# Wide matrix products and a new order of the last rounds in an attention decode kernel

## The chip, the cores and the metric

One core of a Trainium2 chip. The metric is the device time of one launch in microseconds; lower is better. A core has a matrix engine (PE, with its weight loads shown as PEld), a vector engine (DVE), an activation engine (ACT), and a queue (SP) that issues the DMAs here. 16 DMA engines carry the data.

## What is computed

A decode step for 4 batch rows (B = 4, one token each, D = 512): a layer norm modulated by a condition, grouped-query attention over a cache, a gated residual, then a second modulated norm and a small mixing network with its own gate. All numbers are float32.

```python
mod = (_silu(c) @ w_mod).reshape(c.shape[0], 6, 1, -1)
sa, ca, ga, sb, cb, gb = ...                   # six parts of mod
h = _layernorm(x) * (1 + ca) + sa
q = (h @ wq)                                    # 32 heads of 128, 8 key heads
p = softmax(q k^T / sqrt(128))                  # 4096 cached keys per batch row and key head
x = x + ga * ((p v) @ wo)
h = _layernorm(x) * (1 + cb) + sb
u = gelu(_layernorm(h) * w1 + b1)               # 512 channels x 1792
x = x + gb * (u @ w2 + b2)
```

## The kernel before

The 4 x 8 pairs of batch row and key head make 32 *rounds* (`NS = 32`; round i belongs to batch row i // 8 and head i % 8). Each needs a key tile `k` and a value tile `v` of 2 MB, [128 x 4096] floats. All big tiles live in one ring of five places (`ring`), so a load can be issued when the tile five loads earlier has been read. SP takes the loads in program order; each waits there for its place. The last three value tiles come in pieces (`load_v`), the last in four. The output projection's weights `wo` stay in SBUF, one tile for each head.

The order of the work on each engine is the order in which it is written (`manual_schedule`); an instruction that waits holds up everything behind it on its engine. A round consists of:
- `scores(i)`: eight products of 512 columns into `s`, then on DVE the row maximum `m`.
- `colmax(i)` and `expo(i)`: `m` is transposed (`pm`), reduced (`mx`), spread to all partitions (`pb`, `nm`); ACT makes the exponentials `p` and their row sums `l`.
- `transposes(i)`: eight transposes of `p`, a product `pl` that adds the row sums, then on DVE the copy `pT` and the scale `sel`.
- `values(i)`: 32 products of 32 output rows and 128 columns into `pv`. The four column strips of PE work side by side. Then DVE copies `pv` to `po`.
- `project_a(i)`: one product of `po` and `sel` (`pt`), copied by DVE to `oT`.
- `project_b(i)`: 16 products of 128 columns with `wo` into `pa`; DVE adds it to `acc`.

In iteration i of the main loop the two loads come first, then `transposes(i+1)`, `project_a(i-1)`, `scores(i+2)`, `project_b(i-1)`, `colmax` and `expo` of i+2, a step of the epilogue, and `values(i)`. The epilogue of a batch row (residual, norms, the mixing network by `expand` on DVE, a gelu on ACT, `contract` on PE) is a generator that is advanced by `next(epi)` in the rounds of the next row. `mod(t)` makes a part of the modulation with 64 products; `fold_gate` multiplies the gate into the weights of the last head. The last batch row has no following rounds: `finish` does its epilogue at the end, with the last gate (`modmm`) between its steps.

## Time and profile before

| | us |
|---|---|
| median of 3 runs | 396.34 (396.08 to 397.13) |
| profiled execution, span | 394.4 |
| PE busy, DVE busy, ACT busy | 288.9, 151.4, 96.4 |
| time of the main DMA queue, as a share of 16 engines | 93.9% |

The profile is one execution: its span runs from the first to the last instruction; the profile gives no time of its own for that execution beside its span, and the median of the runs is 1.9 us above it. Times in the views are microseconds from the start of the span. PE works on several products at once, so its busy time is not its load.

### The profile page before, as it was taken

How to read it: one execution, taken by the hardware profiler on the slowest of the kernel's cores; microseconds unless marked ns; L12 is line 12 of the kernel's file. 1: busy time of each engine (PE TensorE's matmuls, PEld its weight loads, DVE VectorE, ACT ScalarE, POOL GpSimd, SP SyncE). 2: the span in 40 equal slices, each digit the busy share in tenths (PEclk: the TensorE clock that was granted, in tenths of full speed). 3: DMA queues.
4: the chain of work that ended last, by engine and by line, in shares of the span. 5: the costliest groups of instructions: out<-in, count | busy, mean ns of one | idle time of the engine just before them, and what ended most of it. 6: DMA issues, size and time to landing. Idle time of an engine off the chain costs nothing.

```text
span 394.4 us, 11762 instructions
## 1 busy us (share of the span) xinstructions
PE 288.9 (73%) x5414; PEld 194.4 (49%) x5414; DVE 151.4 (38%) x487; ACT 96.4 (24%) x119; POOL 0.7 (0%) x6
## 2 busy tenths in 40 slices
PE   0976785539967586778677787779776787897884
PEld 0122444408745444556455455557544464675763
DVE  4222222203222232556432334546323345763266
ACT  1001111101110111136641011348411010685125
POOL 0000000000000000000000000000000000000000
PEclk9989689959999889999999899989999898999999
DMA  8999999999999999999999999999999999999700
GB/s 321 425 430 437 431 419 433 420 430 433 429 420 432 429 429 429 427 432 429 429 421 429 430 434 429 424 425 431 432 429 427 425 429 434 427 425 417 289 8 2
DMA packets 12720, 158.08 MB, mean 401 GB/s; under 512 B 1516, under 2 KB 1532, under 8 KB 1920
## 3 DMA queue, kind: packets, MB, share of 16 engines
q1 hardware_dynamic: 12672, 157.34, 93.9%
q8 instruction: 42, 0.69, 0.6%
q14 instruction: 6, 0.05, 0.0%
HBM read 157.32 MB, written 0.01 MB: 399 GB/s over the span
## 4 chain that ended last, share of the span: by engine, by line
DMA 56%; PE 29%; DVE 8%; ACT 4%; issue 1%; SPq 0%; ACTq 0%; DVEq 0%
DMA k<-in_kT 43%; DMA v<-in_v 11%; PE s L205 10%; PE pv L254 5%; DVE m L208 3%; PE s L126 2%; PE s L235 2%; DMA sm<-in_small 2%; PE py L359 2%; DVE u L354 1%; PE pa L282 1%; ACT uu L414 1%; PE pm L190 1%; ACT p L228 1%; PE qs L141 1%
## 5 line engine op out<-in xcount | busy, mean ns | idle before, releaser
L205 PE MATMUL s<-k,QT 128*32 128x512 f32 x512 | 74.0, 703 | 40.3 <-DMA k<-in_kT 40.2
L228 ACT ACTIVATE p<-s,nm 128x1024 f32<-128x1024 f32 x32 | 35.6, 1114 | 234.5 <-DVE nm L225 234.5
L208 DVE TENSOR_REDUCE m<-s 128x1 f32<-128x1024 f32 x32 | 39.2, 1225 | 101.5 <-PE s L205 101.5
L254 PE MATMUL pv<-v,pT 128*32 128x128 f32 x2048 | 64.5, 277 | 5.6 <-DMA v<-in_v 4.5
L254 PEld LDWEIGHTS pv<-v,pT 128*32 128x32 f32 x2048 | 56.2, 111 | 7.6 <-DMA v<-in_v 5.3
L205 PEld LDWEIGHTS s<-k,QT 128*32 128x32 f32 x512 | 14.7, 119 | 66.4 <-DMA k<-in_kT 41.4
L282 PEld LDWEIGHTS pa<-wo,oT 128*32 128x32 f32 x992 | 30.2, 116 | 22.3 <-issue 21.2
L235 PE MATMUL s<-ident,p 128*128 128x128 f32 x256 | 36.4, 286 | 0.7 <-ACT p L228 0.4
L282 PE MATMUL pa<-wo,oT 128*32 128x128 f32 x992 | 34.6, 282 | 0.8 <-DVE oT L271 0.8
L235 PEld LDWEIGHTS s<-ident,p 128*128 128x128 f32 x256 | 28.6, 145 | 6.9 <-issue 6.3
L259 DVE COPY po<-pv 128x128 f32<-128x128 f32 x32 | 9.3, 290 | 41.9 <-PE pv L254 41.9
L354 DVE TENSOR_SCALAR u<-hb,wr,sm 128x512 f32<-128x512 f32 x42 | 20.0, 542 | 2.5 <-PE py L359 2.2
L214 PE MATMUL pm<-ident,m 128*1 128x128 f32 x32 | 8.7, 271 | 16.7 <-DVE m L208 16.7
L379 ACT ACTIVATE u<-u 128x1024 f32<-128x1024 f32 x21 | 20.9, 1047 | 0.1
L238 DVE COPY pT<-s 128x128 f32<-128x128 f32 x32 | 9.3, 290 | 24.8 <-PE s L235 23.6
L223 PE MATMUL pb<-neg,mx 1*32 1x1 f32 x256 | 7.6, 176 | 13.3 <-DVE mx L216 13.3
L214 PEld LDWEIGHTS pm<-ident,m 128*1 128x1 f32 x32 | 2.5, 79 | 28.8 <-DVE m L208 28.8
L126 PE MATMUL s<-wm,sT 128*4 128x512 f32 x16 | 9.6, 771 | 9.7 <-DVE sT L114 9.7
L269 PE MATMUL pt<-sel,po 128*128 128x4 f32 x64 | 11.8, 254 | 4.5 <-DVE po L259 2.9
L228 ACT ACT_TABLE_LOAD x9 | 11.5, 1283 | 13.2 <-DVE nm L225 13.1
L223 PEld LDWEIGHTS pb<-neg,mx 1*32 1x32 f32 x256 | 4.9, 103 | 19.5 <-DVE mx L216 19.5
L359 PE MATMUL py<-u,sm 128*32 128x128 f32 x336 | 11.6, 276 | 2.9 <-ACT u L379 2.9
(114 smaller groups left out, 233.1 us busy)
## 6 DMA issues: line engine op xcount, KB each, us to landing
k<-in_kT SPq DMA_DIRECT2D x32, 2048.0 KB, 22.6
v<-in_v SPq DMA_DIRECT2D x29, 2048.0 KB, 22.5
wq<-in_wq SPq DMA_DIRECT2D x4, 2048.0 KB, 18.0
wo<-in_wo SPq DMA_DIRECT2D x8, 1024.0 KB, 23.1
v<-in_v SPq DMA_DIRECT2D x5, 1024.0 KB, 19.0
wm<-in_wmod SPq DMA_DIRECT2D x2, 2048.0 KB
wm<-in_wmod SPq DMA_DIRECT2D x2, 1024.0 KB, 16.4
v<-in_v SPq DMA_DIRECT2D x1, 512.0 KB, 20.2
```

The lines of the kernel that those rows point to most:

```text
L126: mm(s0[0:B, t * D:(t + 1) * D], sT[:, k, :], wm01[:, t, k, :], start=(k == 0), stop=(k == 3))
L205: mm(s[32 * c:32 * c + 32, n * 512:(n + 1) * 512], QT[:, b, h, :], KT[i][:, (n * 4 + c) * 512:(n * 4 + c + 1) * 512], start=True, stop=True)
L208: dv.tensor_reduce(m, s, axis=AX.X, op=OP.max)
L223: mm(pb[32 * c:32 * c + 32, :], mx, neg1, start=True, stop=True)
L228: nc.scalar.activation(p, s, AF.Exp, bias=nm, accum_out=l)
L235: nc.tensor.transpose(pt[:, k, :], p[:, k * P:(k + 1) * P], ident)
L254: mm(pv[32 * c:32 * c + 32, :], pTs[i % 2][:, k, c, :], VT[i][:, k * 4 + c, :], start=(k == 0), stop=(k == 7))
L269: mm(pt, po, sel, start=True, stop=True)
L282: mm(pa[32 * c:32 * c + 32, :], oT[:, g:g + 1].to_broadcast([P, 32]), wo_t[h][:, g, c * P:(c + 1) * P], start=(g == 0 and not folded), sto ...
L354: dv.tensor_scalar(u[:, e, :], hb, wr[:, j:j + 1], b1[:, j:j + 1], op0=OP.mult, op1=OP.add)
L359: mm(py[32 * c:32 * c + 32, :], w2[:, j:j + 1].to_broadcast([P, 32]), u[:, e, c * P:(c + 1) * P], start=(j == 0), stop=(j == NF - 1))
L379: nc.scalar.activation(u, u, AF.Gelu_apprx_tanh)
```

## The change

- `values` uses 16 products of 256 columns (two value rows at once), `project_b` four of 512 for the first three batch rows, `contract_wide` 14 of 512 for the first two; what then stands in four groups of rows is added up by `fold_groups`, four small products. `project_a` has two products, since `po` has 256 columns. The last round keeps narrow products (`values_last`), and so does `project_b` in the last batch row.
- All four batch rows share one 128-partition layout, eight rows each (`sT8`, `rows`, `8 * b`), so that `mod`, `modmm` and `px` need a quarter of the products.
- `colmax` reduces to four copies of the maximum at once, and `expo` has one spreading product for four.
- An iteration begins with `scores(i+2)`; `values(i)` is cut in two halves around `expo`; the epilogue's steps are placed anew.
- `load_k(31)` goes in front of `load_v(28)`, and the last four rounds are written out. There `scores(31)` stands in front of `transposes(30)`; the gate is multiplied into the weights of the last two heads in three places; the expansion and gelu of the third row's last six slices stand around `values(28)` and `values(29)`, and their contraction right in front of `finish`.
- The output goes out as four DMAs for two.

The diff without its set-up of constants:

```diff
--- before.py
+++ after.py
...
@@ -184,15 +190,15 @@
         if i == NS - 1:
             load_wm(5)
 
-    def modmm(pm, t, steps):
-        for b, k in steps:
+    def modmm(pm, t):
+        for k in range(4):
             for c in range(4):
-                mm(pm[32 * c:32 * c + 32, b, :], sT[:, k, b:b + 1].to_broadcast([P, 32]),
+                mm(pm[32 * c:32 * c + 32, :], sT8[:, k].rearrange("p b r -> p (b r)"),
                    WM[t][:, k, c * P:(c + 1) * P], start=(k == 0), stop=(k == 3))
 
     def mod(t):
-        pm = ps_e.tile([P, B, P], F32, name=f"pm{t}", tag="e")
-        modmm(pm, t, [divmod(e, 4) for e in range(4 * B)])
+        pm = ps_e.tile([P, P], F32, name=f"pm{t}", tag="e")
+        modmm(pm, t)
         return pm
 
     S, SEL, SP = {}, {}, {}
@@ -212,15 +218,15 @@
         s, m = S[i]
         pm = ps_m.tile([1, P], F32, name="pm", tag="m")
         nc.tensor.transpose(pm, m, ident)
-        mx = wk.tile([1, 32], F32, name="mx")
-        dv.tensor_reduce(mx, pm.rearrange("o (c r) -> o r c", c=4), axis=AX.X, op=OP.max)
+        mx = wk.tile([1, 4, 32], F32, name="mx")
+        dv.tensor_reduce(mx, pm.rearrange("o (c r) -> o r c", c=4).unsqueeze(1).to_broadcast([1, 4, 32, 4]),
+                         axis=AX.X, op=OP.max)
         S[i] = [s, mx]
 
     def expo(i):
         s, mx = S[i]
         pb = ps_m.tile([P, 1], F32, name="pb", tag="m")
-        for c in range(4):
-            mm(pb[32 * c:32 * c + 32, :], mx, neg1, start=True, stop=True)
+        mm(pb, mx.rearrange("o c r -> o (c r)"), neg1, start=True, stop=True)
         nm = wk.tile([P, 1], F32, name="nm")
         dv.tensor_copy(nm, pb)
         p = wk.tile([P, 1024], F32, name="p", tag="p")
@@ -235,38 +241,54 @@
             nc.tensor.transpose(pt[:, k, :], p[:, k * P:(k + 1) * P], ident)
         pl = ps_m.tile([P, 1], F32, name="pl", tag="m")
         mm(pl, grp, l, start=True, stop=True)
-        dv.tensor_copy(pTs[i % 2][:, :, :, 0:REP],
-                       pt.rearrange("p k (c r) -> p k c r", c=4)[:, :, :, 0:REP])
+        if i == NS - 1:
+            dv.tensor_copy(pTl[:, :, :, 0:REP], pt.rearrange("p k (c r) -> p k c r", c=4)[:, :, :, 0:REP])
+        else:
+            dv.tensor_copy(pTs[i % 3][:, :, 0:2 * REP].rearrange("p k (c r) -> p k c r", c=2),
+                           pt.rearrange("p k (h c r) -> p (k h) c r", h=2, c=2)[:, :, :, 0:REP])
         rl = wk.tile([P, 1], F32, name="rl")
         dv.reciprocal(rl, pl)
-        sel = wk.tile([P, REP], F32, name="sel", bufs=3)
-        dv.tensor_scalar(sel, sel0, rl, None, op0=OP.mult)
+        sel = wk.tile([P, 2 * REP], F32, name="sel", bufs=4)
+        dv.tensor_scalar(sel, sel8, rl, None, op0=OP.mult)
         SEL[i] = sel
 
     PV = {}
 
     def values(i, ks):
         if ks[0] == 0:
-            PV[i] = ps_v.tile([P, DH], F32, name="pv")
+            PV[i] = ps_v.tile([P, 2 * DH], F32, name="pv", tag="pv")
+        pv = PV[i]
+        for k in ks:
+            q = k % 4
+            mm(pv[32 * q:32 * q + 32, :], pTs[i % 3][:, k, :],
+               VT[i][:, k * 2:(k + 1) * 2, :].rearrange("p j d -> p (j d)"), start=(k < 4), stop=(k >= 12))
+        if ks[-1] == 15:
+            po = wk.tile([P, 2 * DH], F32, name="po")
+            dv.tensor_copy(po, pv)
+            SP[i] = (SEL.pop(i), po)
+
+    def values_last(i, ks):
+        if ks[0] == 0:
+            PV[i] = ps_v.tile([P, DH], F32, name="pvl", tag="pv")
         pv = PV[i]
         for k in ks:
             for c in range(4):
-                mm(pv[32 * c:32 * c + 32, :], pTs[i % 2][:, k, c, :], VT[i][:, k * 4 + c, :],
+                mm(pv[32 * c:32 * c + 32, :], pTl[:, k, c, :], VT[i][:, k * 4 + c, :],
                    start=(k == 0), stop=(k == 7))
-        if ks[-1] < 7:
-            return
-        po = wk.tile([P, DH], F32, name="po")
-        dv.tensor_copy(po, pv)
-        SP[i] = (SEL.pop(i), po)
+        if ks[-1] == 7:
+            po = wk.tile([P, DH], F32, name="po")
+            dv.tensor_copy(po, pv)
+            SP[i] = (SEL.pop(i), po)
 
     ACC = {}
-
     OT = {}
 
     def project_a(i):
         sel, po = SP.pop(i)
         pt = ps_m.tile([P, REP], F32, name="pt", tag="m")
-        mm(pt, po, sel, start=True, stop=True)
+        n = po.shape[-1] // DH
+        for c in range(n):
+            mm(pt, po[:, c * DH:(c + 1) * DH], sel[:, c * REP:(c + 1) * REP], start=(c == 0), stop=(c == n - 1))
         oT = wk.tile([P, REP], F32, name="oT")
         dv.tensor_copy(oT, pt)
         OT[i] = oT
@@ -274,39 +296,45 @@
     def project_b(i, pa=None):
         b, h = divmod(i, HKV)
         oT = OT.pop(i)
-        folded = pa is not None
-        if not folded:
-            pa = ps_m.tile([P, P], F32, name="pa", tag="m")
-        for g in range(REP):
-            for c in range(4):
-                mm(pa[32 * c:32 * c + 32, :], oT[:, g:g + 1].to_broadcast([P, 32]),
-                   wo_t[h][:, g, c * P:(c + 1) * P], start=(g == 0 and not folded), stop=(g == REP - 1))
-        if folded:
-            return
+        if b < B - 1:
+            pa = ps_m.tile([P, D], F32, name="pa", tag="m")
+            for g in range(REP):
+                mm(pa[32 * g:32 * g + 32, :], oT[:, g:g + 1].to_broadcast([P, 32]), wo_t[h][:, g, :],
+                   start=True, stop=True)
+        else:
+            if pa is None:
+                pa = ps_m.tile([P, P], F32, name="pq", tag="m")
+            for g in range(REP):
+                for c in range(4):
+                    mm(pa[32 * c:32 * c + 32, :], oT[:, g:g + 1].to_broadcast([P, 32]),
+                       wo_t[h][:, g, c * P:(c + 1) * P], start=(g == 0 and h < HKV - 1),
+                       stop=(g == REP - 1 and h != HKV - 2))
+            if h >= HKV - 2:
+                return
         if h == 0:
-            ACC[b] = wk.tile([P, P], F32, name="acc")
+            ACC[b] = wk.tile(list(pa.shape), F32, name="acc", tag="acc", bufs=1)
             dv.tensor_copy(ACC[b], pa)
-        elif h < HKV - 1:
+        else:
             dv.tensor_add(ACC[b], ACC[b], pa)
-            if h == HKV - 2:
-                ap_ = wk.tile([P, P], F32, name="ap")
-                dv.tensor_mul(ap_, ACC.pop(b), prep[:, 1, b])
-                dv.tensor_add(ap_, ap_, prep[:, 0, b])
-                EP[b] = ap_
-        else:
-            x1 = XK[:, b]
-            dv.tensor_mul(x1, pa, prep[:, 1, b])
-            dv.tensor_add(x1, x1, EP.pop(b))
-
-    EP = {}
+
+    def fold_groups(pool, acc, tag):
+        pc = pool.tile([P, P], F32, name="pc", tag=tag)
+        for c in range(4):
+            mm(pc[32 * c:32 * c + 32, :], first, acc[:, c * P:(c + 1) * P], start=True, stop=True)
+        return pc
+
+    def residual(x1, pc):
+        dv.tensor_mul(x1, pc, prep[:, 1])
+        dv.tensor_add(x1, x1, prep[:, 0])
+
...
@@ -359,49 +388,72 @@
                 mm(py[32 * c:32 * c + 32, :], w2[:, j:j + 1].to_broadcast([P, 32]),
                    u[:, e, c * P:(c + 1) * P], start=(j == 0), stop=(j == NF - 1))
 
+    def contract_wide(py, u, js):
+        for e, j in enumerate(js):
+            q = j % 4
+            mm(py[32 * q:32 * q + 32, :], w2[:, j:j + 1].to_broadcast([P, 32]), u[:, e, :],
+               start=(j < 4), stop=(j >= NF - 4))
+
     def epilogue(b):
-        stm = stats(XK[:, b])
+        residual(XK[:, b], fold_groups(ps_e, ACC.pop(b), "e"))
+        stm = stats(XK[:, b], b)
         yield
         h1, stm = adaln(b, gather(stm))
         yield
         pst = gather(stm)
-        hb, wr = affine(pst, bcast(h1))
-        py = None
+        hb, wr = affine(pst, bcast(h1, b))
         done = []
-        for group in ((0, 1, 2), (3, 4), (5, 6)):
-            for u, js in done:
-                contract(py, u, js)
-            done = []
-            for j2 in group:
+
+        def activate(*pairs):
+            for j2 in pairs:
                 js = (2 * j2, 2 * j2 + 1)
                 u = up.tile([P, 2, D], F32, name="u")
                 expand(u, hb, wr, js)
                 nc.scalar.activation(u, u, AF.Gelu_apprx_tanh)
                 done.append((u, js))
+
+        activate(0, 1)
+        yield
+        wide = b < B - 2
+        py = ps_e.tile([P, D if wide else P], F32, name="py", tag="e")
+
+        def consume():
+            while done:
+                (contract_wide if wide else contract)(py, *done.pop(0))
+
+        consume()
+        activate(2, 3)
+        yield
+        consume()
+        yield
+        activate(4, 5)
+        yield
+        if wide:
+            consume()
+        activate(6)
+        yield
+        consume()
+        if wide:
+            yw = wk.tile([P, D], F32, name="yw", tag="yw", bufs=1)
+            dv.tensor_copy(yw, py)
+            py = fold_groups(ps_e, yw, "e")
+        else:
             yield
-            if py is None:
-                py = ps_e.tile([P, P], F32, name="py", tag="e")
-        for u, js in done:
-            contract(py, u, js)
-            if b == B - 2:
-                yield
         dv.tensor_scalar(ZK[:, b], py, b2, None, op0=OP.add)
         yield
 
...
@@ -413,26 +465,31 @@
                 expand(u, hb, wr, js)
                 nc.scalar.activation(u, u, AF.Gelu_apprx_tanh)
             contract(py, u, js)
-            if j == 0:
-                modmm(pg, 5, gate[12:])
         next(epi)
-        dst = out.rearrange("b (c n) -> c b n", c=4)
+        dv.tensor_mul(osb[:, :B - 1], ZK, pg.unsqueeze(1).to_broadcast([P, B - 1, P]))
+        dv.tensor_add(osb[:, :B - 1], osb[:, :B - 1], XK[:, :B - 1])
         gbl = cst.tile([P, P], F32, name="gbl")
-        dv.tensor_copy(gbl, pg[:, b])
-        dv.tensor_mul(osb[:, :B - 1], ZK, pg[:, :B - 1])
-        dv.tensor_add(osb[:, :B - 1], osb[:, :B - 1], XK[:, :B - 1])
-        nc.sync.dma_start(dst[:, :B - 1], osb[0:P:32, :B - 1])
+        dv.tensor_copy(gbl, pg)
+        dst = out.rearrange("b (c n) -> b c n", c=4)
+        for e in range(B - 1):
+            nc.sync.dma_start(dst[e], osb[8 * e:P:32, e])
         dv.scalar_tensor_tensor(osb[:, b], py, b2, gbl, op0=OP.add, op1=OP.mult)
         dv.tensor_add(osb[:, b], osb[:, b], XK[:, b])
-        nc.sync.dma_start(dst[:, B - 1:], osb[0:P:32, B - 1:])
-
-    def fold_gate():
+        nc.sync.dma_start(dst[b], osb[8 * b:P:32, b])
+
+    def spread_gate():
         pgb = ps_m.tile([P, 4, P], F32, name="pgb", tag="m")
         for c in range(4):
-            mm(pgb[:, c, :], ident[:, 32 * c:32 * c + 1].to_broadcast([P, P]), prep[:, 1, B - 1],
-               start=True, stop=True)
-        for g in range(REP):
-            dv.tensor_mul(wo_t[HKV - 1][:, g], wo_t[HKV - 1][:, g], pgb.rearrange("p c n -> p (c n)"))
+            e = 32 * c + 8 * (B - 1)
+            mm(pgb[:, c, :], ident[:, e:e + 1].to_broadcast([P, P]), prep[:, 1], start=True, stop=True)
+        gate = wk.tile([P, D], F32, name="gate", tag="yw", bufs=1)
+        dv.tensor_copy(gate, pgb.rearrange("p c n -> p (c n)"))
+        return gate
+
+    def fold_gate(gate, es):
+        for e in es:
+            w = wo_t[HKV - 2 + e // REP][:, e % REP]
+            dv.tensor_mul(w, w, gate)
 
     for i in range(3):
         load_k(i)
@@ -443,28 +500,24 @@
         expo(i)
     transposes(0)
     epi = iter(())
-    for i in range(NS - 1):
-        if i + 3 < NS:
-            load_k(i + 3)
+    for i in range(NS - 4):
+        load_k(i + 3)
+        if i == NS - 5:
+            load_k(NS - 1)
         load_v(i + 1)
-        if i % HKV == 5:
-            next(epi, None)
+        scores(i + 2)
+        if i:
+            project_a(i - 1)
         transposes(i + 1)
         if i:
-            project_a(i - 1)
-        nxt = i + 2 < NS
-        if nxt:
-            scores(i + 2)
-        if i:
             project_b(i - 1)
-        if nxt:
-            colmax(i + 2)
-            expo(i + 2)
-        else:
-            nc.scalar.preload_act_table(AF.Gelu_apprx_tanh)
+        colmax(i + 2)
+        values(i, range(8))
+        expo(i + 2)
+        values(i, range(8, 16))
         if i and i % HKV == 0:
             epi = epilogue(i // HKV - 1)
-        if i % HKV < 5:
+        for _ in range((1, 1, 1, 1, 2, 1, 1, 0)[i % HKV]):
             next(epi, None)
         if 3 <= i <= 5:
             t = i - 1
@@ -474,19 +527,51 @@
                 dv.tensor_scalar(dst, pm, 1.0, None, op0=OP.add)
             else:
                 dv.tensor_copy(dst, pm)
-        values(i, range(8))
-        if i == NS - HKV + 1:
-            fold_gate()
-    project_a(NS - 2)
-    project_b(NS - 2)
-    values(NS - 1, (0, 1, 2, 3, 4, 5))
+        if i == NS - HKV - 2:
+            gate = spread_gate()
+        if i == NS - HKV or i == NS - HKV + 1:
+            e = 3 * (i - NS + HKV)
+            fold_gate(gate, range(e, e + 3))
+    n = NS - 4
+    load_v(n + 1)
+    scores(n + 2)
+    project_a(n - 1)
+    transposes(n + 1)
+    project_b(n - 1)
+    colmax(n + 2)
+    next(epi)
+    expo(n + 2)
+    scores(n + 3)
+    transposes(n + 2)
+    colmax(n + 3)
+    expo(n + 3)
+    values(n, range(16))
+    fold_gate(gate, (6, 7))
+    next(epi)
+    load_v(n + 2)
+    transposes(n + 3)
+    project_a(n)
+    project_b(n)
+    values(n + 1, range(16))
+    next(epi)
+    load_v(n + 3)
+    values(n + 2, range(8))
+    project_a(n + 1)
+    project_b(n + 1)
+    ep = cst.tile([P, P], F32, name="ep")
+    residual(ep, ACC.pop(B - 1))
+    values(n + 2, range(8, 16))
     pgx = ps_s.tile([P, 8, P], F32, name="pgx", tag="s")
-    mm(pgx[:, 4], ident, EP.pop(B - 1), start=True, stop=False)
-    values(NS - 1, (6, 7))
+    x3 = pgx[:, 4]
+    project_a(n + 2)
+    project_b(n + 2, x3)
+    for ks in ((0, 1, 2, 3), (4, 5), (6,), (7,)):
+        values_last(n + 3, ks)
+    mm(x3, ident, ep, start=False, stop=False)
+    project_a(n + 3)
+    project_b(n + 3, x3)
     next(epi)
-    project_a(NS - 1)
-    project_b(NS - 1, pgx[:, 4])
-    finish(B - 1, pgx, pgx[:, 4], epi)
+    finish(B - 1, pgx[:, 0], x3, epi)
 
 
 def kernel(**inputs):
```

53 lines of the change are left out of this document (29 added, 24 removed).

## The prediction

> **What bounds the kernel now.** I read the page first, then the stage table of the last 50 us, then the timeline of the last rounds. Two rows of the page belong together, and a third of the DMA view for the time up to 367.6 us:
>
> ```profile
> q8 instruction: 42, 0.69, 0.6%
> PE 288.9 (73%) x5414; PEld 194.4 (49%) x5414; DVE 151.4 (38%) x487; ACT 96.4 (24%) x119; POOL 0.7 (0%) x6
> q8 instruction: 38, 0.62, 0.6%
> ```
>
> 42 packets of the DMA's traffic are program code (16 KB each, 0.69 MB / 42), 38 of them before 367.6. PE has 10,828 of the 11,762 records, so nearly all of the code is PE's, one packet for some 258 PE records. Next the stage table (busy time of PE, PEld, DVE, ACT, POOL; then granted clock, DMA share, GB/s):
>
> ```profile
> 100.00:150.00 50.00, 34.94 (x768) 26.44 (x760) 13.05 (x40) 4.82 (x8) 0.00 (x0) 0.93 1.01 428
> 343.00:367.60 24.60, 20.42 (x479) 15.62 (x475) 11.88 (x35) 15.32 (x16) 0.00 (x0) 1.00 1.01 423
> 367.60:375.20 7.60, 6.80 (x205) 5.85 (x200) 1.69 (x7) 0.00 (x0) 0.00 (x0) 1.00 0.56 227
> 375.20:394.40 19.20, 12.23 (x302) 9.26 (x294) 12.52 (x43) 8.01 (x9) 0.00 (x0) 0.99 0.01 2
> ```
>
> Until 367.6 us all 16 DMA engines are busy: whatever PE, DVE and ACT do before that costs nothing as long as it keeps up. Then the share is 0.56 for 7.6 us: about half of the engines have finished and the others are late by up to 7.5 us, although all carry the same bytes. The missing part is 0.44 x 7.6 x 16 = 53 engine-us; 38 code packets fall before that, so 1.4 us for each would explain it, if they fall on eight of the engines, five on each. A tile counts as landed only when the slowest engine is done, so these packets set when tiles arrive. From 375.2 no DMA runs and the rest is one chain through PE, DVE and ACT.
>
> So only two things decide: when the last key and value tiles land, and how long the chain from there to the end is. The landing of key tile 28 stands in the chain of waits (305.64 + 23.52 = 329.16):
>
> ```profile
> 305.64 23.52 DMA k<-in_kT
> ```
>
> Behind it come v26, k29, v27 and k30, at 2.097 MB / 428 GB/s = 4.9 us each: k30 lands at 348.7. Its scores start at 349.37:
>
> ```profile
> 349.37 1.92 PE L205 MATMUL s<-k,QT 128*32 128x512 f32 x16
> ```
>
> So the last rounds run right behind the DMA.
>
> **Edits that cost or save nothing.** Wide values, projection, contraction: a round of values is 64 records of 128 columns, the scores 16 records of 512; both are 8,192 columns, and they take 1.93 and 1.92 us (346.14 and 340.73 below). 32 records of 256 are again 8,192 columns: I take no PE time saved, only records. What comes on top each round (two products in the first projection step, a column maximum over 512 instead of 128 elements, an accumulator of 512) is up to 1 us of DVE and 0.3 us of PE. Rounds have 9.8 us (two tiles) and DVE is 38% busy, so the DMA covers it; with that cover gone it would be 1 us in each of 31 rounds. The gate products shrink from 64 to 16 and stand beside DVE chains in the finish. At the start DVE adds two small copies and half a microsecond of memsets; it waits 3.66 us there for the first data:
>
> ```profile
> 8.98 0.17 DVE L111 TENSOR_SCALAR sg<-sg 128x16 f32<-128x16 f32 x1 [3.66 <-ACT sg L110]
> ```
>
> Scores in front of transposes: scores wait for the key tile as before, and what is behind them on PE belongs to older rounds; hidden by the same cover.
>
> k31 in front of v28: SP issues it when k28's place is free, long before; v28 comes 4.9 us later, and values(28) wait for it. That matters in the chain below.
>
> **The code packets.** Counting PE's queue in the changed program gives 1,740 matrix instructions for 2,857: values 2,048 records become about 1,056, projection 1,024 become 448, gate and modulation 512 become 128, and so on. That makes 6,384 PE records for 10,828, at 258 a packet 25 for 42; some 22 for 38 before the loads end. The latest engine gets three instead of five: 2 x 1.4 = 2.7 us (rounded down). Bounds: nothing (the lateness has another cause) to 4.1 (three fewer). Fewest assumptions carry 2.7, since both the size and the half fit the table. So k30 lands at 346.0, k31 at 350.9, v28 at 355.8, v29 at 360.7, v30 at 365.6, and the last of v31 at 370.5.
>
> **The chain of the last rounds.** The rows of one round of before, and the end:
>
> ```profile
> 340.41 0.39 PE L269 MATMUL pt<-sel,po 128*128 128x4 f32 x2 [0.82 <-DVE po L259]
> 340.73 1.92 PE L205 MATMUL s<-k,QT 128*32 128x512 f32 x16
> 340.84 0.16 DVE L271 COPY oT<-pt 128x4 f32<-128x4 f32 x1
> 342.47 1.06 PE L282 MATMUL pa<-wo,oT 128*32 128x128 f32 x32
> 342.72 1.22 DVE L208 TENSOR_REDUCE m<-s 128x1 f32<-128x1024 f32 x1 [1.72 <-PE s L205]
> 343.86 0.28 DVE L290 TENSOR_TENSOR acc<-acc,pa 128x128 f32<-128x128 f32 x1
> 344.00 0.27 PE L214 MATMUL pm<-ident,m 128*1 128x128 f32 x1 [0.47 <-DVE m L208]
> 344.64 0.24 PE L223 MATMUL pb<-neg,mx 1*32 1x1 f32 x8 [0.37 <-DVE mx L216]
> 344.81 1.52 PE L359 MATMUL py<-u,sm 128*32 128x128 f32 x48
> 345.94 1.92 DVE L354 TENSOR_SCALAR u<-hb,wr,sm 128x512 f32<-128x512 f32 x4 [0.84 <-PE py L359]
> 346.14 1.93 PE L254 MATMUL pv<-v,pT 128*32 128x128 f32 x64
> 348.00 1.09 PE L235 MATMUL s<-ident,p 128*128 128x128 f32 x8
> 348.14 0.29 DVE L259 COPY po<-pv 128x128 f32<-128x128 f32 x1 [0.28 <-PE pv L254]
> 349.08 0.36 PE L269 MATMUL pt<-sel,po 128*128 128x4 f32 x2
> 349.20 0.29 DVE L238 COPY pT<-s 128x128 f32<-128x128 f32 x1 [0.77 <-PE s L235]
> L435 DVE TENSOR_TENSOR wo<-wo,pgb 128x512 f32<-128x512 f32 x4 | 2.5, 682 | 0.3 <-PE pgb L432 0.3
> L476 DVE COPY prep<-pm 128x512 f32<-128x512 f32 x2 | 1.4, 692 | 7.4 <-PE pm L190 7.4
> 376.11 1.08 PE L282 MATMUL pgx<-wo,oT 128*32 128x128 f32 x32 [0.25 <-DVE oT L271]
> 377.26 0.30 DVE L307 BATCH_NORM_STATS2 st<-pgx 128x6 f32<-128x128 f32 x1 [1.20 <-PE pgx L282]
> 377.83 0.40 PE L315 MATMUL pst<-stm,ones 128*128 128x24 f32 x2 [0.31 <-DVE stm L309]
> ```
>
> From starts of neighbours: scores hold PE 1.74 and give the maximum 1.99 after their start; the maximum is ready for PE 1.28 later; values 1.85 (copy out 2.0); transposes with their sum 1.07; projection step two 0.90 (its result 1.15 after its start, 376.11 to 377.26); step one 0.3 for one product, I take 0.6 for two; one expansion 0.48; a small DVE step 0.2; the copy of 256 columns 0.36 (0.29 for 128, 0.69 for 512); a gate multiplication 0.61 in a row.
>
> Scores(30) start at 346.0. PE then does step one, transposes and step two of older rounds, to 350.3; the sum into the accumulator is done at 350.8, since DVE takes it ahead of the column maximum; that has 512 elements now, 0.69 by the row of L476: 351.5. Scores(31) start at 351.6, the maximum is out at 354.9, three small steps and the column maximum of 0.7 follow, 356.2, and values(28) start at 356.4 (v28 landed at 355.8). Their copy begins at 358.4. Now DVE's queue decides: copy 0.36, two gate multiplications 1.2, four expansions 1.9, and only then the copy of the last transposes, two small steps, and the copy out of step one: 362.8. PE's queue has transposes and step one behind values, is through at 359.9, and waits 2.9 us at step two of head 28; behind it stand values(29), whose tile is there since 360.7. Values(29) 363.7, first half of values(30) 365.5. DVE has copy and two expansions before the next copy: step two (29) at 367.25, second half of values(30) 368.15, copy, step one, copy: step two (30) 370.6, values(31) 371.5 (all landed), copy 373.55, step one 373.9, step two (31) at 374.55. Before: 376.11. Gain 1.55.
>
> Then the finish. The contraction that stood beside the copy of before now comes whole, 24 products, between step two and the sums of the norm: 0.9 + 1.33 (344.81 to 346.14) + 0.33 = 2.56 after step two starts, for 1.72 (377.83): loss 0.84. The rest of the finish keeps its chain (DVE, then ACT). At its end SP has three output issues instead of one ahead of the last:
>
> ```profile
> 390.36 0.67 SPq L424 DMA_DIRECT2D out<-osb  x1
> 391.48 0.29 DVE L426 TENSOR_TENSOR osb<-osb,xk 128x128 f32<-128x128 f32 x1
> 391.79 0.55 SPq L427 DMA_DIRECT2D out<-osb  x1
> ```
>
> Three of 0.55 to 0.67 end at 392.0 instead of 391.0: 0.2 lost. Sum: -1.55 + 0.84 + 0.2 = -0.5.
>
> **The clock.** The wait of 2.9 us has a second price:
>
> ```profile
> 308.47 3.62 PE L205 MATMUL s<-k,QT 128*32 128x512 f32 x16 [1.52 <-DMA k<-in_kT]
> 305.10:308.51 3.41, 1.89 (x36) 1.61 (x27) 0.95 (x5) 0.00 (x0) 0.00 (x0) 1.00 1.04 437
> 308.51:311.92 3.41, 3.41 (x20) 0.84 (x24) 0.00 (x0) 0.00 (x0) 0.00 (x0) 0.50 0.97 418
> 325.58:328.99 3.41, 1.74 (x17) 1.68 (x15) 3.10 (x9) 0.00 (x0) 0.00 (x0) 1.00 0.97 408
> 328.99:332.40 3.41, 3.29 (x17) 0.80 (x21) 0.30 (x2) 0.00 (x0) 0.00 (x0) 0.50 1.03 442
> 332.40:394.00 61.60, 48.38 (x1130) 37.41 (x1122) 33.30 (x108) 29.45 (x32) 0.00 (x0) 1.00 0.65 271
> ```
>
> A stretch of 3.41 us with PE half idle is followed by one at clock 0.50, in which scores took 3.62 us for 1.92. From 332.4 on before had none. In after the wait takes most of such a stretch; the next one then costs half of the work in it, at most 1.7 us, nothing where the stretches cut the wait in the middle. I take 0.7. So the profiled execution would be 394.4 - 0.5 + 0.7 = 394.6; the median of the runs lies 1.9 above the span, 396.34 + 0.2: 396.5, no change within 0.3% (1.2 us, about what a measurement of this kernel can tell from none).
>
> **The rivals.**
> Slower, landing: the lateness of half the engines is not from code packets. Then k30 lands at 348.7 as before, and as the chain follows that landing step by step, all of the 2.7 comes back: 396.5 + 2.7 = 399.2. It decides from a landing of k30 later than 347.0. For it: no row gives the engine of a code packet. Against: size and half fit. Chance 0.14.
> Slower, clock: PE idles 2 us before scores(30) as well, and two stretches run at 0.50: another 1.7, 398.2. For it: 305.10, where 1.5 us idle were enough. Chance 0.14.
> Faster: wide records pay a fixed part once where narrow ones pay it four or two times. A narrow record of values is issued every 30 ns (1.93 us / 64); if half of that were fixed, a round of 32 wide records took 1.45. The chain from 356.4 holds values(28), (29) and (30): 1.4 less, and a shorter hole for the clock to fall into: 396.5 - 1.4 - 0.4 = 394.7. For it: the row of values alone cannot tell columns from a fixed part. Against: scores, with records four times as long, need the same time for the same columns. Chance 0.27. The Trainium skill, "TensorE: Matmul & The Clock Gate", section on the back-to-back issue gap, gives about 81 ns a matmul of 128 columns and 131 ns of 512 for streams with weight loads, so that wide ones would cost less than half by column. By that rule values would save about as much as this rival says; the rows of values and scores here, 1.93 and 1.92 us for the same columns, disagree.
> Clock stays: PE is not throttled by a wait of 2.9 us; 396.34 - 0.5 = 395.8. The rows above speak against it, since half-idle stretches were enough. Chance 0.15. The Trainium skill, "TensorE: Matmul & The Clock Gate", section on why this matters for kernels, asks for no idle gap of more than about 3 us between bursts; by that rule the clock would stay. This trace disagrees: an idle time of 1.52 us was followed by 0.50.
>
> **How the numbers follow.** Forecast 0.30 and clock-stays 0.15 are within 0.3%: 0.45. Faster 0.27, slower 0.28. The forecast's own range is 395.3 to 397.6. The range for 8 in 10 takes in most of the faster case and the clock rival and leaves out the far half of the landing rival: 394.4 to 398.6.
>
> **What would show it.** Code packets near 25, and the half-share end of the DMA 5 us or shorter: landing right. A DVE queue with multiplications and four expansions ahead of the copy of step one, and some 2.9 us of PE waiting at step two of head 28: chain right. Clock 0.50 after it: price right. Wrong if scores(30) start later than 347.0, or if values(31) wait for their tile. The 48 records of contraction ahead of the norm's sums must show 0.8 us more between the last step two and the sums.

## The result: slower by 1.2%, and the profile after

The changed kernel takes 401.13 us (median of 4 runs, 401.06 to 401.34), the kernel before 396.21 us: 1.0123 times as long, 95% interval 1.0109 to 1.0138. The forecast was 396.5, in a range of 394.4 to 398.6. The profiled execution has a span of 399.4 us for 394.4.

The page of the changed kernel first. PE's records and the code packets fell as counted:

```profile
span 399.4 us, 7327 instructions
PE 303.4 (76%) x3180; PEld 153.4 (38%) x3180; DVE 180.7 (45%) x494; ACT 99.2 (25%) x121; POOL 0.7 (0%) x6
q1 hardware_dynamic: 12680, 157.34, 93.3%
q8 instruction: 25, 0.41, 0.4%
```

The stage table of the changed kernel (busy time of PE, PEld, DVE, ACT, POOL; granted clock, DMA share, GB/s):

```profile
100.00:343.00 243.00, 199.99 (x1997) 100.52 (x1989) 122.81 (x329) 67.74 (x82) 0.00 (x0) 0.92 1.01 426
343.00:370.00 27.00, 21.22 (x311) 13.34 (x303) 13.24 (x35) 12.78 (x14) 0.00 (x0) 0.94 1.01 419
371.00:375.90 4.90, 3.84 (x81) 2.80 (x77) 1.62 (x7) 1.06 (x1) 0.00 (x0) 1.00 0.44 179
```

The half-share end of the DMA has shrunk from 7.6 to 4.9 us, as forecast for fewer code packets. But it does not begin earlier: 371.0 for 367.6, so the fast engines are late now. Over the long middle the rate is 426 GB/s. The same row of the kernel before, and the main queue's on its page (packets, MB, share of 16 engines):

```profile
100.00:343.00 243.00, 184.30 (x3611) 130.23 (x3607) 99.22 (x325) 63.31 (x79) 0.00 (x0) 0.96 1.01 428
```

```profile
q1 hardware_dynamic: 12672, 157.34, 93.9%
```

There is a sharper number than the rounded rates: the time that all packets of the main queue took. Before it is 0.939 x 394.4 x 16 = 5,925 engine-us, after 0.933 x 399.4 x 16 = 5,962, for the same 157.34 MB. Spread over 16 engines, that is 37 / 16 = 2.3 us more for the same bytes. (A share is rounded to 0.1%, so each sum is good to some 3 engine-us.)

The timeline of the last rounds of the changed kernel:

```profile
348.46 1.92 PE L211 MATMUL s<-k,QT 128*32 128x512 f32 x16 [1.54 <-DMA k<-in_kT]
359.13 1.93 PE L263 MATMUL pv<-v,pT 128*32 128x256 f32 x32
361.47 1.28 DVE L492 TENSOR_TENSOR wo<-wo,gate 128x512 f32<-128x512 f32 x2
362.68 1.91 DVE L383 TENSOR_SCALAR u<-hb,wr,sm 128x512 f32<-128x512 f32 x4
365.24 1.93 PE L309 MATMUL pq<-wo,oT 128*32 128x128 f32 x32 [2.58 <-DVE oT L293]
366.94 2.72 PE L263 MATMUL pv<-v,pT 128*32 128x256 f32 x32
370.22 1.07 PE L263 MATMUL pv<-v,pT 128*32 128x256 f32 x16 [0.56 <-DVE po L267]
379.31 1.08 PE L309 MATMUL pgx<-wo,oT 128*32 128x128 f32 x32 [0.25 <-DVE oT L293]
380.21 1.49 PE L388 MATMUL py<-u,sm 128*32 128x128 f32 x48
381.96 0.40 PE L343 MATMUL pst<-stm,ones 128*128 128x24 f32 x2
385.31 1.75 PE L365 MATMUL py<-h,ident 128*128 128x128 f32 x8
394.86 1.72 SPq L475 DMA_DIRECT2D out<-osb  x3
396.68 0.51 SPq L478 DMA_DIRECT2D out<-osb  x1
```

And the clock around it (PE busy, granted clock, DMA share, GB/s):

```profile
361.89:365.30 3.41, 0.83 (x12) 0.98 1.01 420
365.24:368.70 3.46, 3.46 (x52) 0.52 1.02 414
385.70:392.40 6.70, 4.74 (x59) 0.50 0.00 0
```

Scores(30) start at 348.46, not 346.0. The forecast wait at step two of head 28 is there (2.58 us, behind two multiplications and four expansions on DVE), and the half clock behind it, which made step two 1.93 us for 1.08 and values(29) 2.72 (values(28), ahead of it, took 1.93). The last step two starts at 379.31 for 376.11 before. The sums of the norm come 2.65 us behind it for 1.72, since the contraction stands between. And a second stretch at half clock lies in the finish, where before had none that PE worked in: the spreading products take 1.75 us for the 1.14 of before:

```profile
381.19 1.14 PE L336 MATMUL py<-h,ident 128*128 128x128 f32 x8
```

### The profile page after: what moved, and what is told of

Its sections match the earlier page's. It is cut to its first block, busy times and chain, and to the rows that moved or that the text cites. A ratio compares the mean times of both kernels' runs of the same rounds, so it can differ in the third digit from the quotient of the medians.

```text
span 399.4 us, 7327 instructions
## 1 busy us (share of the span) xinstructions
PE 303.4 (76%) x3180; PEld 153.4 (38%) x3180; DVE 180.7 (45%) x494; ACT 99.2 (25%) x121; POOL 0.7 (0%) x6
## 3 DMA queue, kind: packets, MB, share of 16 engines
q1 hardware_dynamic: 12680, 157.34, 93.3%
## 4 chain that ended last, share of the span: by engine, by line
DMA 68%; PE 24%; DVE 4%; ACT 2%; issue 1%; SPq 1%; ACTq 0%
DMA k<-in_kT 40%; DMA v<-in_v 22%; PE s L211 7%; DMA wq<-in_wq 6%; PE pv L263 5%; PE s L241 2%; PE pa L302 2%; PE pt L291 2%; ACT uu L466 1%; PE pq L309 1%; PE pb L229 1%; PE py L388 1%; DVE mx L222 1%; PE pgx L309 1%; PE qs L146 0%
## 5 line engine op out<-in xcount | busy, mean ns | idle before, releaser
L263 PE MATMUL pv<-v,pT 128*32 128x256 f32 x992 | 67.2, 390 | 6.6 <-DMA v<-in_v 6.0
L263 PEld LDWEIGHTS pv<-v,pT 128*32 128x32 f32 x992 | 27.8, 111 | 23.0 <-PE pm L220 6.3
L291 PEld LDWEIGHTS pt<-sel,po 128*128 128x128 f32 x126 | 18.5, 211 | 30.9 <-issue 23.8
L302 PE MATMUL pa<-wo,oT 128*32 128x512 f32 x192 | 29.9, 699 | 0.5 <-DVE oT L293 0.5
L267 DVE COPY po<-pv 128x256 f32<-128x256 f32 x31 | 13.2, 425 | 28.4 <-PE pv L263 28.4
L222 DVE TENSOR_REDUCE mx<-pm 1x128 f32<-1x512 f32 x32 | 21.5, 672 | 0.7 <-PE pm L220 0.7
L291 PE MATMUL pt<-sel,po 128*128 128x4 f32 x126 | 21.3, 274 | 0.5 <-DVE po L267 0.5
L318 DVE TENSOR_TENSOR acc<-acc,pa 128x512 f32<-128x512 f32 x21 | 14.4, 688 | 13.4 <-PE pa L302 13.4
L229 PEld LDWEIGHTS pb<-neg,mx 1*128 1x128 f32 x64 | 9.6, 186 | 17.2 <-DVE mx L222 15.5
L229 PE MATMUL pb<-neg,mx 1*128 1x1 f32 x64 | 12.3, 259 | 4.2 <-DVE mx L222 4.2
```

Of the source, the lines that this page charges most:

```text
L222: dv.tensor_reduce(mx, pm.rearrange("o (c r) -> o r c", c=4).unsqueeze(1).to_broadcast([1, 4, 32, 4]), axis=AX.X, op=OP.max)
L229: mm(pb, mx.rearrange("o c r -> o (c r)"), neg1, start=True, stop=True)
L263: mm(pv[32 * q:32 * q + 32, :], pTs[i % 3][:, k, :], VT[i][:, k * 2:(k + 1) * 2, :].rearrange("p j d -> p (j d)"), start=(k < 4), stop=(k ...
L291: mm(pt, po[:, c * DH:(c + 1) * DH], sel[:, c * REP:(c + 1) * REP], start=(c == 0), stop=(c == n - 1))
L302: mm(pa[32 * g:32 * g + 32, :], oT[:, g:g + 1].to_broadcast([P, 32]), wo_t[h][:, g, :], start=True, stop=True)
L318: dv.tensor_add(ACC[b], ACC[b], pa)
```

## The experiments

Each kernel was timed against the kernel before on the same chip; medians of before were 395.67 to 396.16 there, and 396.21 beside the changed kernel. So the difference of two medians from different sessions is uncertain by some half a microsecond; where that matters, the difference of their distances from before (each kernel's median less that of the kernel before in its own session) is given too.

**The gate and the expansions later** (from the changed kernel):

```diff
-    fold_gate(gate, (6, 7))
-    next(epi)
     load_v(n + 2)
     transposes(n + 3)
     project_a(n)
+    fold_gate(gate, (6, 7))
+    next(epi)
     project_b(n)
```

> The changed kernel with one difference: the last two gate multiplications and the four expansions of the third row stand behind the copy of step one of head 28 on DVE, not ahead of it. My theory: the hole of 2.58 us at step two of head 28 goes, and with it the stretch at half clock behind it (step two 1.93 for 1.08 us, values(29) 2.72 for 1.93). Then step two of head 28 starts near 362.8 instead of 365.24, the last step two near 375.2 instead of 379.31, bound by the last piece of v31 (373.4): some 4 us gone, time near 397. Rival A (the hole only moves, since the 3.1 us of DVE work now delay the copy of values(29)): half of it back, 399. Rival B (the time was lost because the landings did not come earlier, so the order of the tail is worth nothing): 401.1.

397.26 us, 1.0051 of before (1.0032 to 1.0070). Its timeline:

```profile
363.13 1.08 PE L309 MATMUL pq<-wo,oT 128*32 128x128 f32 x32 [0.29 <-DVE oT L293]
364.03 1.91 PE L263 MATMUL pv<-v,pT 128*32 128x256 f32 x32
366.69 1.07 PE L263 MATMUL pv<-v,pT 128*32 128x256 f32 x16 [0.75 <-DVE po L267]
375.79 1.08 PE L309 MATMUL pgx<-wo,oT 128*32 128x128 f32 x32 [0.25 <-DVE oT L293]
```

The hole is 0.29 us, both operations behind it run at full clock, and the last step two is 3.5 us earlier. Of the moved 3.1 us of DVE work little came back: values(30) wait 0.75 us for the copy of values(29), where they waited 0.56 in the changed kernel. So DVE's order in this one place was worth 3.9 us by the medians (3.3 by the distances from before), some 1.7 of them through the clock.

**The contraction behind the gate products** (from the changed kernel):

```diff
     project_b(n + 3, x3)
-    next(epi)
     finish(B - 1, pgx[:, 0], x3, epi)
...
         modmm(pg, 5)
+        next(epi)
         h1, stm = adaln(b, pst)
```

> The changed kernel with one difference: the contraction of 24 products stands behind the gate products in the finish, where PE waits for DVE, not ahead of the norm's sums. My theory: the sums start 1.72 instead of 2.65 us after the last step two, 0.93 us gone; and as PE is busier between 383 and 385, the stretch at half clock from 385.7 may go too, in which the spreading products took 1.75 for 1.14 us: another 0.6. Time 400.2 if only the first holds, 399.6 with both. Rival (the finish is bound by ACT's gelus, not by the sums): 401.1.

399.91 us, 1.0103 (1.0084 to 1.0122). Its timeline:

```profile
379.43 1.08 PE L309 MATMUL pgx<-wo,oT 128*32 128x128 f32 x32 [0.25 <-DVE oT L293]
381.15 0.40 PE L343 MATMUL pst<-stm,ones 128*128 128x24 f32 x2 [0.31 <-DVE stm L337]
384.51 1.14 PE L365 MATMUL py<-h,ident 128*128 128x128 f32 x8
```

The sums come 1.72 us behind step two again, and the spreading products run at full clock. Between them that is 1.5 us by the rows; the median fell by 1.2 (0.7 by the distances from before). The interval overlaps that of the changed kernel (1.0109 to 1.0138), so the gain is shown by the rows and not by the runs alone. The stretch at half clock did not go: it starts at 387.20 in this profile, behind the spreading products.

**Narrow values in all rounds** (from the changed kernel):

```diff
         for k in ks:
-            q = k % 4
-            mm(pv[32 * q:32 * q + 32, :], pTs[i % 3][:, k, :], VT[i][:, k * 2:(k + 1) * 2, :]..., ...)
+            for c in range(4):
+                mm(pv[32 * c:32 * c + 32, :], pTs[i % 3][:, k, c, :], VT[i][:, k * 4 + c, :],
+                   start=(k == 0), stop=(k == 7))
```

> The changed kernel with narrow values in all rounds (64 records of 128 columns instead of 32 of 256). PE's records grow by 1,984, so there should be some 33 code packets for 25. The theory of the prediction (code packets set when tiles land): one packet more on each late engine, k30 lands 1.4 us later, time 402.5. Rival (the sum of all engines' traffic sets it, the packets only decide which engine is late): the same landing of k30 near 348.4 within 0.5, time 401.1. Third (wide products save PE or DVE time by themselves): time above 402 with the landing where it was.

401.56 us, 1.0150 (1.0135 to 1.0165). 32 code packets on its page, and in its timeline scores(30) begin when k30 lands:

```profile
q8 instruction: 32, 0.52, 0.5%
```

```profile
349.90 1.92 PE L210 MATMUL s<-k,QT 128*32 128x512 f32 x16 [1.53 <-DMA k<-in_kT]
```

Seven packets more put the landing 1.44 us later (348.46 in the changed kernel), the 1.4 that the prediction gives one packet on each late engine. So the landing moves with the number of code packets; something else took the gain away. The time rose by 0.4 us (1.0 by the distances from before) and missed the 402.5 that was expected: the last step two starts at 379.73, only 0.42 us later than in the changed kernel. In the narrow tail step one has one product for two (0.39 us for 0.61), and step two of head 28 ran at full clock (1.08 us), though values(29) did not (3.44 us).

**Wide values alone** (from the kernel before):

```diff
+        if i < NS - 1:
...
+            for k in range(16):
+                q = k % 4
+                mm(pv[32 * q:32 * q + 32, :], pTs[i % 2][:, k, :], VT[i][:, k * 2:(k + 1) * 2, :]..., ...)
...
-        mm(pt, po, sel, start=True, stop=True)
+        for c in range(n):
+            mm(pt, po[:, c * DH:(c + 1) * DH], sel[:, c * REP:(c + 1) * REP], ...)
```

> The kernel before with wide values in rounds 0 to 30 and nothing else of the change. Code packets near 34 for 42. The theory of the prediction: k30 lands 1.4 us earlier (347.3 for 348.7), time 395.0. Rival (landings do not follow the code packets): 348.5 or later, time 396.2. If wide products themselves cost DMA rate, the rate from 100 to 300 us falls from 428 to 426 GB/s as it did with the whole change, and the time rises to 397.

396.24 us, 1.0012 (0.9999 to 1.0026): no gain that the runs can tell, and no loss of rate. Its code packets, its stage table, and scores(30) and its last step two in the timeline:

```profile
q8 instruction: 35, 0.57, 0.5%
```

```profile
100.00:343.00 243.00, 191.53 (x2938) 120.17 (x2930) 104.03 (x326) 63.33 (x79) 0.00 (x0) 0.94 1.01 429
```

```profile
348.47 1.92 PE L207 MATMUL s<-k,QT 128*32 128x512 f32 x16
375.21 1.08 PE L299 MATMUL pgx<-wo,oT 128*32 128x128 f32 x32 [0.25 <-DVE oT L288]
```

Its k30 is issued at 325.1 us and lands 22.2 us later, at 347.3, as the theory had it; that of before is issued at 325.0 and lands 23.6 us later, at 348.6. In its profiled execution scores(30) and the last step two are each 0.9 us earlier than before (349.37 and 376.11). But the expected time of 395.0 was missed: the median shows nothing of it. The rate of 429 clears the wide products of the loss: it belongs to something else in the change. One thing that the changed kernel and the three built on it share, and that the two with 428 and 429 lack, is where the ring lies in SBUF. The constants in front of it shrank by 2,944 bytes a partition (`prep` -6,144, `pT` +2,048, `sT8` +512, `rows` +128, `ep` +512), 11.5 times 256; so its places begin at 110,464 instead of 113,408, half a step off the multiple of 256. (These are the addresses of the program's allocation; no view shows an address.)

**The ring moved back, and before's ring moved off** (two kernels with the same line; in the changed kernel it brings the ring to 110,592 = 432 x 256, in the kernel before to 113,536):

```diff
+    pad = cst.tile([P, 32], F32, name="pad")
+    dv.memset(pad, 0.0)
```

> The changed kernel with one unused tile of 128 bytes a partition in the constants, so that the five places of the ring begin at a multiple of 256 bytes in SBUF as they did before the change (before: 113,408 = 443 x 256; changed: 110,464, a multiple of 128 only; here: 110,592). Theory: the DMAs into the shifted ring ran at 425 to 427 GB/s for 428 to 430, and that, not the code packets, kept the landings where they were. Then the rate from 100 to 343 us is 428 to 430 here, scores(30) start near 346.0 instead of 348.5, as the prediction had it, and the time falls by 2.4 to 398.7. Rival A (the loss of rate comes from the wide products or from the new order of the work): rate 426, scores(30) at 348.5, time 401.1. Rival B (rate comes back, but the tail is bound by something later): scores(30) at 346.0 and time above 400.

398.25 us, 1.0058 (1.0030 to 1.0085). Page, stage table and timeline of it:

```profile
span 395.4 us, 7328 instructions
q1 hardware_dynamic: 12680, 157.34, 93.5%
q8 instruction: 25, 0.41, 0.4%
```

```profile
100.00:343.00 243.00, 199.39 (x2002) 98.95 (x2000) 123.02 (x331) 67.72 (x82) 0.00 (x0) 0.92 1.01 430
```

```profile
345.93 1.92 PE L213 MATMUL s<-k,QT 128*32 128x512 f32 x16 [0.61 <-DMA k<-in_kT]
362.71 1.08 PE L311 MATMUL pq<-wo,oT 128*32 128x128 f32 x32 [2.59 <-DVE oT L295]
366.06 1.07 PE L265 MATMUL pv<-v,pT 128*32 128x256 f32 x16 [0.55 <-DVE po L269]
375.16 1.08 PE L311 MATMUL pgx<-wo,oT 128*32 128x128 f32 x32 [0.25 <-DVE oT L295]
```

The packets take 0.935 x 395.4 x 16 = 5,915 engine-us, the rate is 430, and k30 lands for scores at 345.93; the forecast was 346.0.

> The kernel before with the same unused tile, which here shifts the ring off the multiple of 256 bytes (113,536). Theory (place in SBUF): the rate falls from 428 to 426 GB/s, the last key tile and the last values land 1.5 to 4 us later, time 397.2 to 399.5 for 395.7. Rival (place does not matter): 395.7.

398.65 us, 1.0059 (1.0038 to 1.0080), with nothing added to the kernel before but an unused tile. Its page, stage table and timeline:

```profile
span 396.8 us, 11763 instructions
q1 hardware_dynamic: 12672, 157.34, 93.8%
```

```profile
100.00:343.00 243.00, 186.78 (x3591) 133.15 (x3582) 98.70 (x323) 62.51 (x79) 0.00 (x0) 0.94 1.01 425
```

```profile
351.66 1.92 PE L207 MATMUL s<-k,QT 128*32 128x512 f32 x16
```

5,955 engine-us, 425 GB/s, scores(30) 2.3 us later than before's 349.37; its k30 is issued at 327.6 and lands 23.9 us later, at 351.5 for 348.6. The place alone does it, in both directions. The tile moves everything allocated behind the constants, but of that only the ring is filled by loads.

**A shift of 64 bytes** (the kernel before, the same tile with half the size; ring at 113,472):

```diff
+    pad = cst.tile([P, 16], F32, name="pad")
+    dv.memset(pad, 0.0)
```

> The kernel before with an unused tile of 64 bytes, so that the ring begins at 113,472, a multiple of 64 only. With the shift of 128 bytes the rate fell to 424 to 427 GB/s and the time rose by 0.6%. Theory 1 (only a start at a multiple of 256 is free, any other costs the same): rate 425 to 426, time 398.2 to 399. Theory 2 (the smaller the power of two, the dearer): rate under 424, time over 400. Theory 3 (it is 128 bytes in particular that hurts): rate 428, time 396.

399.02 us, 1.0080 (1.0057 to 1.0102); 0.938 x 397.1 x 16 = 5,960 engine-us. That fits theory 1, at the upper end of its times: off the multiple of 256, 64 and 128 bytes cost the same as far as these runs can tell. The Trainium skill, "DMA: Bandwidth & Descriptors", section on how a descriptor splits into AXI transactions, says that a piece which does not start at a multiple of 256 bytes needs a partly wasted transaction in front, in beats of 32 bytes; it speaks of reads. By that rule a row of 16 KB (512 beats) would cost 4 beats more at a shift of 128, an estimated 0.8%, and 2 more at 64, 0.4%. The direction agrees; the measured 0.5 to 0.6% (5,955 and 5,960 for 5,925) is between the two and, within the rounding, the same for both.

**Three differences together, and the tile order taken back** (from the changed kernel: the pad of 128 bytes, the gate and expansions later, the contraction behind the gate products; the second kernel also this):

```diff
-        if i == NS - 5:
-            load_k(NS - 1)
         load_v(i + 1)
+        if i == NS - 5:
+            load_k(NS - 1)
```

> The changed kernel with three differences: the ring at a multiple of 256 bytes, the gate multiplications and four expansions behind the copy of step one of head 28, and the contraction of 24 products behind the gate products in the finish. If the three losses are apart from each other they add up: 2.4 + 3.9 + 1.2 of 401.1, that is 393.6. If the tail without the hole is bound by the landings of the last value pieces, which come 2 us earlier with the rate, 394.5. Rival (they are the same loss counted twice): 397.

393.55 us, 0.9954 of before (0.9934 to 0.9974): faster than both kernels. The three losses are apart from each other: by the distances from before the ring is worth 2.4 us, the gate 3.3 and the contraction 0.7, 6.4 in all, and the three together 7.1. That the median meets the expected 393.6 so closely is chance, since the terms are not known to a tenth.

> The same as the one with three differences, but with the last key tile behind the value tile of head 28 again, as before the change. Theory: k31 lands 4.9 us later, scores(31) stand ahead of the transposes of 30 and of values(28) on PE, so PE waits some 4 us there and the chain behind it is later by 2 to 4 us: 396 to 398. Rival (the last value pieces bind, the order of the two tiles is worth nothing): the same time as without.

398.91 us, 1.0073 (1.0048 to 1.0097), 5.4 more than without. The key tile in front of the value tile is worth more than I expected, given the written-out tail.

**The tile order alone** (from the kernel before):

```diff
-        if i + 3 < NS:
+        if i + 3 < NS - 1:
             load_k(i + 3)
+        if i == NS - 5:
+            load_k(NS - 1)
         load_v(i + 1)
```

> The kernel before with the last key tile loaded in front of the value tile of head 28 and nothing else of the change; the rounds keep their order, so scores(31) stand behind values(28) on PE. Theory: values(28) wait for v28, 4.9 us later than before, and scores(31) gain nothing from the earlier tile, since they stand behind them: the time rises by 0.5 to 3, 396.2 to 398.7 for 395.7. The tile order pays only with the written-out tail. Rival (the earlier key tile pays by itself): under 395.

400.79 us, 1.0115 (1.0094 to 1.0136), a bigger loss than expected. Its timeline shows why:

```profile
359.05 3.56 PE L254 MATMUL pv<-v,pT 128*32 128x128 f32 x64 [4.52 <-DMA v<-in_v]
364.34 1.92 PE L205 MATMUL s<-k,QT 128*32 128x512 f32 x16
```

PE waits 4.52 us for v28, then pays 3.56 us for 1.93 at half clock, and only then comes to scores(31), whose tile has long been there (before: 359.35). The same reordering of two loads costs 4.6 us with one order of PE's queue and brings 5.4 with the other.

**PE kept busy in its waits** (the changed kernel with the ring at a multiple of 256, and products nobody reads: 14 ahead of `project_b(n)`, 7 and 10 in the finish):

```diff
+    def warm(pw, n):
+        for _ in range(n):
+            mm(pw, ident, ident, start=True, stop=True)
...
     project_a(n)
+    pgx = ps_s.tile([P, 8, P], F32, name="pgx", tag="s")
+    warm(pgx[:, 6], 14)
     project_b(n)
```

> The changed kernel with the ring at a multiple of 256 bytes and with 31 products of the identity with itself, whose results nobody reads: 14 in front of step two of head 28, where PE waits 2.6 us, 7 and 10 in the waits of the finish (0.134 us each by the transposes' row, 1.9, 0.9 and 1.3 us). Nothing on the path moves; only PE's idle time is filled. Theory (idle PE is what halves the clock): the hole's stretch at half clock never comes, the finish's comes less or later, the median falls from the 398.25 of the aligned kernel to its fastest runs or below, 395.6 to 396.5, and the runs spread by less than 2 us instead of 4.9. Rival (the half clock has another cause, or the products delay the chain): 398.2 or above with the same spread.

397.60 us, 1.0037 (1.0023 to 1.0052), all six runs between 397.40 and 398.33, where the ten of the kernel without the products lie between 396.54 and 401.41. Its stage table:

```profile
344.00:396.00 52.00, 43.54 (x776) 32.68 (x768) 28.18 (x85) 21.84 (x24) 0.00 (x0) 1.00 0.51 213
```

The clock is 1.00 from 344 us on. The median missed the expectation: I took 0.134 us for a product, from transposes, which are one record each; these are two:

```profile
360.78 3.37 PE L197 MATMUL pgx<-ident 128*128 128x128 f32 x28
364.08 1.08 PE L315 MATMUL pq<-wo,oT 128*32 128x128 f32 x32
```

14 of them took 3.37 us instead of 1.9 and made step two wait for PE; those in the finish were too many as well. So filling the waits took the half clock away and narrowed the runs: PE's idle time does bring the half clock here. The median fell by only 0.65 us (1.1 by the distances from before), since the products cost part of what they saved. That the clock is the whole of the spread is not shown: the mean clocks of the ten runs without them (0.890 to 0.922) do not order their times.

**The fastest version** (the three differences, ten such products in the finish only, and one output issue on ACT's queue):

```diff
+        warm(pw, 10)
...
-            nc.sync.dma_start(dst[e], osb[8 * e:P:32, e])
+            (nc.scalar if e == 1 else nc.sync).dma_start(dst[e], osb[8 * e:P:32, e])
```

> The kernel with three differences (ring at a multiple of 256 bytes, gate multiplications and expansions later, contraction behind the gate products), and two more: 10 identity products in the wait of the finish, and the second output issue on ACT's queue, so that SP has two instead of three ahead of the last (0.55 us each; the last waited 0.3 us for them). Expected: 0.2 to 0.6 below the 393.55 of the one with three differences, 393.0 to 393.4. Rival (the tail end is bound by DVE and ACT alone): 393.5.

393.24 us, 0.9937 of before (0.9914 to 0.9960). Its last DVE step and output issues:

```profile
387.04 1.18 SPq L483 DMA_DIRECT2D out<-osb  x2
388.15 0.29 DVE L485 TENSOR_TENSOR osb<-osb,xk 128x128 f32<-128x128 f32 x1
388.47 0.51 SPq L486 DMA_DIRECT2D out<-osb  x1
```

The last issue starts 0.03 us behind the DVE step (388.44), where in the changed kernel it started 0.30 behind it (396.38). Against the 393.55 without these two the difference is within what these runs can tell. Six of its eight runs lie between 393.02 and 393.46, and two took 395.45 and 395.77, so some of the spread is left.

## Why the prediction was wrong

By the profiled execution the forecast was 394.6 and 399.4 came: 4.8 too little. Where they lie, step by step:

- **Landing: mechanism right, one assumption wrong, 2.46 us.** 25 code packets as counted; a half-share end of 4.9 us, as forecast. With the ring at a multiple of 256, k30 landed at 348.6 with 42 packets (349.3 in the kernel with the tile order alone), at 347.3 with 35, and scores(30) started at 345.93 with 25, for a forecast of 346.0; with the ring off that multiple seven packets were worth 1.44 us. What a packet costs its engine is less sure than the 1.4 of the prediction: its own time by the page before is 0.6% x 394.4 x 16 / 42 = 0.9 us, and no run shows what the rest is. The step that failed is the one that took before's 428 GB/s over to the changed program and costed its constants at "half a microsecond of memsets". They move the ring by 11.5 x 256 bytes, and the loads need 2.3 us more of each engine, on average. The landing rival's condition came true (348.46 is later than 347.0), but not its reason: the lateness did shrink with the code packets.
- **Clock in the hole: mechanism right, 0.96 us short.** Step two (28) and values(29) lost 0.85 and 0.81 us (1.08 and 1.91 with the gate later), 1.66 together, near the bound of 1.7; I took 0.7. The rival that the clock stays falls with it: the wait was 2.58 us. But half idle, then half clock is not the whole rule: in the kernel with the ring moved back PE was busy for 1.52 of the 3.41 us from 360.82, and the next stretch ran at 1.00, while 2.04 of the 3.40 us from 377.9 were followed by 0.50. What decides is open.
- **Chain from scores(30) to the last step two: 0.64 us short.** 28.55 were forecast, 30.85 measured, of which 1.66 are the clock. In the kernel with the ring moved back, whose hole was followed by no half clock in its profile, it is 375.16 - 345.93 = 29.23. Up to the hole the chain fits: step two (28) 16.8 us behind scores(30) in the forecast and 16.78 there. Behind it I missed that `pv` has one place: values(30) wait 0.55 us for the copy of values(29).
- **Finish: 0.74 us short.** The contraction cost 0.93 for 0.84. The half clock at 385.7 was not in the forecast: 0.61 on the spreading products. That is the slower rival's second cold stretch, in another place: it named the wait before scores(30), and the end of the gate products (16 for 64) left PE idle in the finish instead. Three output issues cost 0.3 for 0.2. These rows give 0.8 of the 0.74.
- **Wide products save no PE time: right.** Values are 1.93 us in 32 records of 256 columns as in 64 of 128. The faster rival falls with it.

2.46 + 0.96 + 0.64 + 0.74 = 4.80. With the ring in its old place the kernel's median is 398.25, inside the range but above its middle, for the reasons of the other three.

## What to carry to other kernels

When a kernel is bound by DMA, count the bytes of everything allocated in front of its big tiles: a constant that grows by 128 bytes shifted them off a multiple of 256, which started scores(30) 2.3 us later here and stands in no row of the profile before. Compare the total packet time (share x span x engines) of two profiles of the same bytes; it told of the shift where rates rounded to 426 and 428 barely did. And a transfer order and an instruction order are one decision: the same two loads exchanged cost 4.6 us with one queue on PE and brought 5.4 with another.

## What the hardware showed that was not expected

- The start of a tile in SBUF matters to the DMA that fills it: 5,914 to 5,925 engine-us for 157.34 MB in the kernels whose ring starts at a multiple of 256 bytes, 5,955 to 5,962 in those that start 64 or 128 beside it.
- An idle stretch of PE seems to have a price that differs from run to run: the kernel with the waits left open ran in 396.54 to 401.41 us (ten runs), the one with them filled in 397.40 to 398.33 (six).
